# The kv product of a linear attention on 64x32 tiles of TensorE, and a VectorE transpose in place of picking matmuls

## The chip, the cores and the metric

The kernel runs on one core of a Trainium2 chip. The metric is the time of one execution on the device in microseconds, smaller being better. The kernel before took 177.84 us, the median of 3 runs (177.82 to 178.65).

## The reference

Two blocks read the same layer-normalised tokens and are added to the input: a linear attention with a softmax feature map (A) and a small convolutional MLP mixer (B). There are 2048 tokens of 448 numbers, 16 heads of 28, and a hidden width of 1792. All data are bf16.

```python
x  = A_x
xn = layernorm(x)
out = x + A(xn) + B(xn)

# A: per head h of 16, Dh = 28
q, k, v = split(xn @ wqkv)
pq, pk  = q @ w_phi[h], k @ w_phi[h]
phi_q = concat([softmax(pq), softmax(-pq)])     # 56 features
phi_k = concat([softmax(pk), softmax(-pk)])
kv  = phi_k.T @ v                               # 56 x 28 per head, summed over 2048 tokens
z   = phi_k.sum(over tokens)                    # 56 per head
o   = (phi_q @ kv) / (phi_q @ z + 1e-6)
A   = concat_heads(o) @ wo

# B
h  = gelu(layernorm(xn) @ w1)
hs = concat of four channel groups of h, shifted by 1, -1, 2, -2 tokens, @ w2
x1 = xn + hs
B  = x1 + gelu(layernorm(x1) @ w3) @ w4
```

## The kernel before

Tokens lie in 16 tiles of 128. Every operation goes through a recorder: the program calls `R.mm` (TensorE matmul, line 203), `R.act` (ScalarE, line 211), `R.ew` (an elementwise operation on VectorE or GpSimd, line 215) and `R.dma`, in one order written out by hand, and the recorder gives each engine its own instructions in that order and adds a wait where an operand's last writer or reader is another engine. So the hand-written order is the order on each engine; engines run freely against each other between those waits. `solve` (lines 75 to 149) works out the waits; PSUM is tracked by whole banks, of which there are 8, in pairs that `two(b)` reads as one.

Most matmuls contract over 64 rows and come in pairs: one on array rows 0 to 63 (`LO`), one on rows 64 to 127 (`HI`), into two different banks.

The stages, in the order of TensorE's work:

1. Layer norm, transposes of the normalised tokens, v for tiles 0 to 11, the w1 product with gelu, and the folding of `w_phi` into the weights of q and k. This ends with the fold's copies into `wpq`, before 33 us.
2. A loop of eight passes (`ps` 0 to 7, from about 31.4 to 69 us; pass 3 begins at 45.11 us). A pass makes k's features for two token tiles (`k_pair`, banks 2 and 3), q's features for one of 8 blocks (`q_pair`, banks 0 and 1) and one pair of w2 or v tiles (`w2_pair` or `v_pair`, banks 4 and 5). Each of these has a first and a second half on TensorE, called k first, k second and so on below. ScalarE makes the exponentials of k and q (`k_exp`, `q_exp`, two each), VectorE adds the w2 result to the tokens (`w2_out`), sums k's features (`k_norm`: a reduce and a reciprocal) and in some passes makes layer norm statistics (`w2_norm`); GpSimd scales k's features by the reciprocal (the rest of `k_norm`) and applies the second layer norm (`g_apply`).
3. From 68.97 us on, a list that `play` goes through: w3 with gelu for two blocks of 128 hidden columns at a time (`a(p)` its first half, `b(p)` its second), the last w2 tiles, the query products (`N(i)`, with `kvq` as moving operand), w4 and wo, and the stores.

The kv product is what changes. For each token tile, `kv_tile` issues 16 matmuls into banks 6 and 7 (rows `LO` into bank 6, rows `HI` into bank 7). The stationary operand is 128 columns of `phik`, the features of two heads (plus and minus softmax, 32 columns each); the moving operand is the 62 columns of `vaug` that hold the same two heads' v and a column of ones, so half of what comes out pairs a head with its neighbour and is not used. Two token tiles go in each of passes 3 to 7, between k first and w first: that is where 10 of the 16 tiles are. Tiles 10 to 13 come as `K(10, 11, 12, 13)` after `b(1)`, tiles 14 and 15 before `b(3)`. Then `kv_copy` adds the two banks into `kvT`, and `kv_blocks` issues four matmuls with a picking matrix (`pick`, made in `kv_picks` by GpSimd's fill and four VectorE copies) that move the wanted 32-row blocks to the partitions that the query product needs, and four copies (two on VectorE, two on ScalarE) write them to `kvq`.

The first query product, `N(0)`, comes after `a(6)`.

Of the kernel before, what the change touches and what calls it, by code (L numbers as in the profile page):

```python
# [6 lines left out]
ALU = mybir.AluOpType  # L7
AX = mybir.AxisListType
BF16 = mybir.dt.bfloat16
F32 = mybir.dt.float32  # L10
# [7 lines left out]
class Recorder:  # L18
# [56 lines left out]
    def solve(self):  # L75
        pos = {e: 0 for e in self.ENGS}
        known = {e: {} for e in self.ENGS}
        snap = {}
        writers = {}
        readers = {}  # L80
        waits = []
        self.stream = {e: [] for e in self.ENGS}
        ndma = 0
        tiles = {}
        mode = (None, 0)
        for eng, fn, w, r, dma, tile in self.ops:
            me = (eng, pos[eng])
            src = ("D%d" % ndma, 0) if dma else me
            if dma:
                ndma += 1  # L90
            need = {}

            def want(d, raw):
                for f, i in d.items():
                    if f == eng:
                        if eng in ("PE", "SP"):
                            continue
                        if not raw and eng != "POOL":
                            continue
                    if need.get(f, -1) < i:  # L100
                        need[f] = i

            for k in r:
                if k in writers:
                    want(writers[k], True)
                if self.rows[k[0]][1] and k in readers:
                    want({f: i for f, i in readers[k].items() if f != eng}, False)
            for k in w:
                if k in writers:
                    want(writers[k], False)  # L110
                if k in readers:
                    want(readers[k], False)
            if eng == "PE":
                if tile[1] != mode[0]:
                    mode = (tile[1], mode[1] + 1)
                for k in w:
                    for lo, (i, m) in tiles.setdefault(k, {}).items():
                        if lo != tile[0] and m == mode[1]:
                            need["PE"] = max(need.get("PE", -1), i)
                    tiles[k][tile[0]] = (pos["PE"], mode[1])  # L120
            kn = known[eng]
            todo = []
            for f, i in sorted(need.items(), key=lambda t: -t[1]):
                if kn.get(f, -1) >= i:
                    continue
                todo.append((f, i))
                for g, j in snap[(f, i)].items():
                    if kn.get(g, -1) < j:
                        kn[g] = j
                kn[f] = max(kn.get(f, -1), i)  # L130
            todo = [(f, i) for f, i in todo
                    if not any(f2 != f and snap[(f2, i2)].get(f, -1) >= i for f2, i2 in todo)]
            s = dict(kn)
            s[src[0]] = src[1]
            if not dma:
                s[eng] = pos[eng]
            snap[src] = s
            self.stream[eng].append((fn, todo, src, dma))
            waits.extend(todo)
            pos[eng] += 1  # L140
            for k in r:
                readers.setdefault(k, {})[src[0]] = src[1]
            for k in w:
                writers.setdefault(k, {})[src[0]] = src[1]
        self.marked = {}
        for f, i in set(waits):
            self.marked.setdefault(f, []).append(i)
        for f in self.marked:
            self.marked[f] = {i: n + 1 for n, i in enumerate(sorted(self.marked[f]))}
# [74 lines left out]
def bass_parallel_sum__linear_kernel_hedgehog__mixer_s_mlp__prompt_kernel(  # L224
# [13 lines left out]
    with es:  # L238
        R = Recorder(nc, es)
# [9 lines left out]
        def view(h, cols, dt=BF16, at=0):  # L249
            a = h[:, at // 2:at // 2 + cols * DTB[dt] // 2]  # L250
            return a if dt == BF16 else a.bitcast(dt)
# [38 lines left out]
        bd = view(g_r, D)  # L290
        wphi = view(g_r, NC * DH, at=1024).rearrange("p (c f) -> p c f", c=NC)
        kvq = new("kvq", 8 * 64).rearrange("p (b e) -> p b e", b=8)
        kvT = view(w1_r, 512)
        kvf = view(w1_r, 512, F32, at=1024)
        pick = view(w1_r, 2 * 128, at=3072).rearrange("p (s c) -> p s c", s=2)
        ident = new("ident", 128)
        maskb = new("maskb", CR)
        st = new("st", NT * 8, F32).rearrange("p (t c) -> p t c", t=NT)
# [192 lines left out]
        def two(b):  # L491
            return pairs[b // 2].rearrange("p (b e) -> p b e", b=2)
# [3 lines left out]
        def row_pairs(first, second, start=False):  # L496
            for s, (p, q) in enumerate(zip(first, second)):
                for out, lhs, rhs in (p, q):
                    R.mm(out, lhs, rhs, start and s == 0, False)
# [67 lines left out]
            R.ew(dve, "reciprocal", rk, k)  # L567
            R.ew(pool, "tensor_tensor", ph, ph, rk.unsqueeze(2).to_broadcast([128, 4 * H, DH]), op=ALU.mult)

        def kv_tile(i):  # L570
            def side(k, rows):
                return [(banks[6 + k][:, 64 * n:64 * n + HP + DH + 2],
                         phik[rows[0]:rows[1], i, 4 * n:4 * n + 4, :].rearrange("p g e -> p (g e)"),
                         vaug[rows[0]:rows[1], i, 64 * n:64 * n + HP + DH + 2]) for n in range(8)]
            row_pairs(side(0, LO), side(1, HI), i == 0)

        def kv_picks():
            R.ew(pool, "memset", pick[:, :, :], 0.0)
            for q in range(4):
                r = slice(HP * q, HP * q + HP)  # L580
                R.ew(dve, "tensor_copy", pick[r, q % 2, :].rearrange("p (n e) -> p n e", n=4),
                     ident[r, HP * q:HP * q + HP].unsqueeze(1).to_broadcast([HP, 4, HP]))

        def kv_copy():
            n61 = [a.rearrange("p (n e) -> p n e", n=8)[:, :, 0:HP + DH + 2] for a in (banks[6], banks[7], kvf, kvT)]
            R.ew(dve, "tensor_copy", n61[2], n61[0])
            R.ew(dve, "tensor_tensor", n61[3], n61[1], n61[2], op=ALU.add)

        def kv_blocks():
            kt = kvT.rearrange("p (n h e) -> p n h e", n=8, h=2)  # L590
            for s in range(2):
                for k, lo in enumerate((0, 64)):
                    R.mm(banks[6 + k][:, 256 * s:256 * s + 256].rearrange("p (n e) -> p n e", n=8)[:, :, 0:DH + 1],
                         pick[lo:lo + 64, s, :], kt[lo:lo + 64, :, k, 0:DH + 1], s == 0, False)
            for q in range(4):
                r, h, n = slice(HP * q, HP * q + HP), q % 2, 4 * (q // 2)
                src = banks[6 + h][r, :].rearrange("p (s n e) -> p s n e", s=2, n=8)[:, :, n:n + 4, 0:DH + 1]
                dst = kvq[r, :, HP * h:HP * h + DH + 1].rearrange("p (c s) e -> p s c e", s=2)
                if h:
                    R.act(dst, src, ACT.Copy)  # L600
                else:
                    R.ew(dve, "tensor_copy", dst, src)
# [171 lines left out]
                ln_scale(mv2, rs2, i - 2, 4, 4)  # L774

        kv_ones()
        kv_picks()
        side = [("w", 0), ("v", 12), ("w", 2), ("w", 4), ("v", 14), ("w", 6), ("w", 8), ("w", 10)]
        g_at = {2: (0,), 3: (1,), 4: (2, 3), 6: (4,), 7: (5,)}
        for ps in range(8):  # L780
            k, q = k_pair(2 * ps, 1), q_pair(ps // 2, 2 * (ps % 2), 0)
            kind, i = side[ps]
            w = {"w": w2_pair, "v": v_pair}[kind](i, 2)
            k[0]()
            if ps > 2:
                kv_tile(2 * ps - 6)
                kv_tile(2 * ps - 5)
            w[0]()
            k[1]()
            for s in range(2):  # L790
                k_exp(2 * ps, 1, s)
            q[0]()
            w[1]()
            if kind == "w":
                w2_out(i, 2)
            if kind == "v":
                v_out(i, 2, "DVE" if i == 12 else "ACT")
            q[1]()
            for s in range(2):
                q_exp(2 * ps, 0, s)  # L800
            k_norm(2 * ps)
            if kind == "w" and i < 8:
                w2_norm(i)
            for t in g_at.get(ps, ()):
                g_apply(t)
                g_T(t)
# [5 lines left out]
        def a(p):  # L812
            return (w3p[p][0],)

        def b(p):
            return (w3p[p][1],)
# [5 lines left out]
            return (lambda: (num_tile(i), o_T(i)),)  # L822

        def K(*t):
            return (lambda: [kv_tile(i) for i in t],)

        def w2_last(i):
            wl[i][1]()
# [8 lines left out]
        def A(*t):  # L837
# [1 line left out]

        play([  # L840
            A(6, 7), G(6, 7),
            a(0), (wl[12][0],), b(0), a(1), (w2_last, 12), b(1), K(10, 11, 12, 13),
            a(2), (wl[14][0],), b(2), a(3), K(14, 15), b(3), (kv_copy,),
            a(4), (w2_last, 14), b(4), a(5), (kv_blocks,), b(5),
            a(6), N(0), (w2_norm, 8), b(6), a(7), f(1, 0), b(7), N(1), (w2_norm, 10), A(8, 9, 10, 11),
            a(8), f(2, 0), b(8), G(8, 9), a(9), N(2), (w2_norm, 12), b(9),
            a(10), f(3, 0), b(10), f(4, 0), G(10, 11),
# [50 lines left out]
```

## Time and profile before

| | |
|---|---|
| median of 3 runs | 177.84 us |
| span of the profiled execution, first to last instruction | 175.9 us |
| time of that execution beside its span | not recorded by itself; the median lies 1.9 us above the span |
| TensorE (PE) busy | 170.8 us, 97% |
| VectorE (DVE) | 110.0 us, 63% |
| GpSimd (POOL) | 93.7 us, 53% |
| ScalarE (ACT) | 82.5 us, 47% |
| chain of waits that ended last | TensorE 91%, VectorE 6% |
| granted TensorE clock | 0.999 of full speed |

PE is TensorE's matmuls, PEld its weight loads, which run beside them. A matmul's recorded length holds its way through the array: the 62-column matmul is recorded with 188 ns, though the next on the same rows starts after some 28. What a group of matmuls costs is therefore read from the start of the group to the start of the next one, in the timeline. A timeline row gives the start in us, the length in us, the engine, the line, the operation, output and inputs with their shapes, and in brackets how long the engine had stood idle and for whom. In a shape such as `64*128 64x62`, the first part is the rows and columns of the array that are used, the second the moving operand.

### The profile page before, as it was taken

The numbers are of one execution on the slowest core, as the hardware profiler recorded it, in microseconds if no ns is written. First come the engines' busy times: TensorE is split into PE (matmuls) and PEld (weight loads), VectorE is DVE, ScalarE is ACT, GpSimd is POOL, SyncE is SP. The second block draws the span as 40 slices with busy tenths as digits, with TensorE's granted clock in tenths as the row PEclk, the third lists the DMA queues.
The fourth block names the chain that finished last, engine by engine and source line by source line (L and its number), as shares of the span: only waits on it lengthen the run. The fifth ranks groups of instructions, "written<-read, shape, count | busy, mean of one in ns | idle before, by whom it ended". The sixth has DMA issues, their size and how long they took to land.

```text
span 175.9 us, 5042 instructions
## 1 busy us (share of the span) xinstructions
PE 170.8 (97%) x2198; PEld 94.7 (54%) x2198; DVE 110.0 (63%) x252; ACT 82.5 (47%) x92; POOL 93.7 (53%) x130
## 2 busy tenths in 40 slices
PE   7899999998999999999999999999999999999993
PEld 4466557744565555665554554554545545545551
DVE  4799906699899697615776981644427415474621
ACT  2368874997779877926324422223214222224000
POOL 3666670016799999860358489460620723523740
PEclk9999999999999999999999999999999999999999
DMA  5994158990001120121011372134611310311331
GB/s 172 330 240 79 35 97 255 390 345 15 0 4 30 34 60 4 30 55 39 4 34 40 79 74 59 48 82 89 93 30 57 82 34 0 86 30 30 86 100 34
DMA packets 32981, 14.87 MB, mean 85 GB/s; under 512 B 24704, under 2 KB 32448, under 8 KB 32960
## 3 DMA queue, kind: packets, MB, share of 16 engines
q1 hardware_dynamic: 30192, 12.64, 29.6%
q10 hardware_dynamic: 2768, 1.92, 3.4%
q8 instruction: 17, 0.28, 0.7%
q14 instruction: 4, 0.03, 0.1%
HBM read 7.08 MB, written 1.84 MB: 51 GB/s over the span
## 4 chain that ended last, share of the span: by engine, by line
PE 91%; DVE 6%; issue 1%; POOL 0%; ACT 0%; DVEq 0%
PE bank L203 90%; DVE vaug L215 1%; DVE st L215 1%; DVE ksum L215 1%; PE bank L207 1%; DVE xn L215 1%; DVE mv L215 0%; ACT xnT L211 0%; POOL rs L215 0%; DVE rks L215 0%; DVEq L176 0%; DVE gT L215 0%; POOL mv L215 0%
## 5 line engine op out<-in xcount | busy, mean ns | idle before, releaser
L211 ACT ACTIVATE phik<-bank 128x1024 bf16<-128x1024 f32 (+1 forms) x44 | 42.3, 984 | 62.4 <-PE bank L203 62.4
L203 PE MATMUL bank<-gT,w 64*128 64x512 bf16 x392 | 50.1, 377 | 0.0
L215 DVE TENSOR_TENSOR vaug<-bank,vaug 128x464 f32<-128x464 f32 (+3 forms) x65 | 32.6, 512 | 23.0 <-PE bank L203 21.4
L203 PE MATMUL bank<-w,phik 64*128 64x448 bf16 (+1 forms) x420 | 45.0, 349 | 0.0
L215 POOL TENSOR_TENSOR xnT<-vaug 128x196 bf16<-128x196 f32 (+1 forms) x32 | 18.1, 585 | 46.8 <-DVE vaug L215 46.8
L203 PEld LDWEIGHTS bank<-w,phik 64*128 64x128 bf16 (+1 forms) x420 | 21.7, 94 | 21.2 <-issue 0.4
L215 POOL TENSOR_TENSOR phik<-phik,rks 128x1792 bf16<-128x1792 bf16 x8 | 25.7, 3212 | 10.8 <-DVE rks L215 10.8
L203 PEld LDWEIGHTS bank<-gT,w 64*128 64x128 bf16 x392 | 18.6, 94 | 17.0 <-ACT hi L211 0.3
L215 POOL TENSOR_TENSOR vaug<-xn,xtok 128x448 f32<-128x448 bf16 x16 | 16.2, 1031 | 0.2 <-DVE vaug L215 0.2
L215 DVE TENSOR_REDUCE ksum<-phik 128x64 f32<-128x1792 bf16 x8 | 16.0, 2006 | 0.0
L203 PE MATMUL bank<-w,hT 64*128 64x448 bf16 (+1 forms) x128 | 15.0, 349 | 0.5 <-DVE vaug L215 0.5
L215 DVE RECIPROCAL vaug<-bank 128x16 f32<-128x16 f32 x16 | 4.1, 257 | 18.0 <-PE bank L203 18.0
L203 PE MATMUL bank<-xnT,wpq 64*128 64x512 bf16 x112 | 14.9, 376 | 0.0
L203 PE MATMUL bank<-xnT,w 64*112 64x512 bf16 x112 | 14.8, 380 | 0.0
L203 PE MATMUL bank<-wpk,xnT 64*128 64x448 bf16 x112 | 13.4, 349 | 0.0
L203 PE MATMUL bank<-wo,xnT 64*128 64x448 bf16 (+1 forms) x106 | 13.4, 349 | 0.0
L215 DVE TENSOR_TENSOR xn<-bank,xn 128x512 bf16<-128x512 f32 (+1 forms) x16 | 9.2, 616 | 6.3 <-PE bank L203 6.3
L203 PE MATMUL bank<-wv,xnT 64*128 64x448 bf16 x112 | 13.0, 350 | 0.1
L215 POOL TENSOR_TENSOR rs<-mv,mhalf 128x1 f32<-128x1 f32 (+2 forms) x18 | 12.2, 679 | 1.5
L215 POOL TENSOR_SCALAR g_tok<-xn,rs 128x512 bf16<-128x512 bf16 x16 | 12.1, 767 | 0.2
L211 ACT ACTIVATE xnT<-bank 128x512 bf16<-128x512 bf16 x12 | 7.0, 603 | 6.3 <-PE bank L207 6.3
L215 DVE BATCH_NORM_STATS2 st<-xtok 128x6 f32<-128x448 bf16 x16 | 9.8, 615 | 0.0
(62 smaller groups left out, 168.0 us busy)
## 6 DMA issues: line engine op xcount, KB each, us to landing
w<-in_B_w_dram SPq DMA_DIRECT2D x2, 896.0 KB, 7.1
out_dram<-vaug SPq DMA_DIRECT2D x15, 112.0 KB, 1.9
w<-in_B_w_dram SPq DMA_DIRECT2D x1, 1568.0 KB, 12.0
xtok<-in_A_x_dram ACTq DMA_DIRECT2D x2, 448.0 KB, 7.3
xtok<-in_A_x_dram SPq DMA_DIRECT2D x2, 224.0 KB, 5.7
w<-in_B_w_dram ACTq DMA_DIRECT2D x2, 224.0 KB, 5.8
wo<-in_A_wo_dram SPq DMA_DIRECT2D x2, 224.0 KB, 8.4
w<-in_B_w_dram SPq DMA_DIRECT2D x1, 392.0 KB, 3.8
```

The source lines that it names most:

```text
L203: self.op("PE", lambda e: e.matmul(out, lhsT, rhs, start=start, stop=stop, skip_group_check=True), [out], [lhsT, rhs], tile=self._tile(lhsT))
L207: self.op("PE", lambda e: e.transpose(out, in_, ident), [out], [in_, ident], tile=self._tile(in_))
L211: self.op("ACT", lambda e: e.activation(out, in_, func, **kw), [out], [in_] + aps)
L215: self.op(eng, lambda e: getattr(e, name)(out, *args, **kw), [out], aps)
```

## The change

kv is turned round. v of one head (32 columns with the ones) becomes the stationary operand and the features of the head (64 columns, plus and minus) the moving one. The output of a head is then 32 partitions by 64 columns, and the head's place among the four groups of 32 partitions is chosen so that the query product finds it there. A token tile takes 32 matmuls, each on 64 array rows by 32 array columns: eight different such tiles of the array are used in turn (two halves of the rows, four groups of columns). No output is left unused. The 16 token tiles go in two batches: tiles 0 to 11 before `b(0)`, tiles 12 to 15 before `b(3)`; the loop of passes has no kv any more.

The accumulation no longer starts with a flag: VectorE clears banks 6 and 7 before the loop. After the last tile VectorE adds the two banks, transposes the result in blocks of 32x32 (`transpose`, into `kvX`), and four copies, from SBUF now, write `kvq`. The picking matrix and its matmuls are gone. In the recorder, an engine that writes PSUM now also waits for its own earlier reads of that bank; VectorE's clearing is the only instruction that this touches.

```diff
@@ solve
                 if k in readers:
-                    want(readers[k], False)
+                    want(readers[k], self.rows[k[0]][1])
@@ buffers
-        kvT = view(w1_r, 512)
-        kvf = view(w1_r, 512, F32, at=1024)
-        pick = view(w1_r, 2 * 128, at=3072).rearrange("p (s c) -> p s c", s=2)
+        kvT = view(w1_r, 256)
+        kvX = view(w1_r, 256, at=512)
+        kvf = view(w1_r, 256, F32, at=1024)
@@ kv
-        def kv_tile(i):
-            def side(k, rows):
-                return [(banks[6 + k][:, 64 * n:64 * n + HP + DH + 2],
-                         phik[rows[0]:rows[1], i, 4 * n:4 * n + 4, :].rearrange("p g e -> p (g e)"),
-                         vaug[rows[0]:rows[1], i, 64 * n:64 * n + HP + DH + 2]) for n in range(8)]
-            row_pairs(side(0, LO), side(1, HI), i == 0)
-
-        def kv_picks():
-            R.ew(pool, "memset", pick[:, :, :], 0.0)
+        def kv_tiles(tiles):
+            for i in tiles:
+                for s in range(4):
+                    for k, (lo, hi) in enumerate((LO, HI)):
+                        for q in range(4):
+                            h = 8 * (q // 2) + 2 * s + q % 2
+                            R.mm(banks[6 + k][HP * q:HP * q + HP, 64 * s:64 * s + 64],
+                                 vaug[lo:hi, i, HP * h:HP * h + HP],
+                                 phik[lo:hi, i, 2 * h:2 * h + 2, :].rearrange("p g e -> p (g e)"),
+                                 False, False)
+
+        def kv_copy():
+            R.ew(dve, "tensor_copy", kvf, banks[6][:, 0:256])
+            R.ew(dve, "tensor_tensor", kvT, banks[7][:, 0:256], kvf, op=ALU.add)
+            R.ew(dve, "transpose", kvX, kvT)
             for q in range(4):
                 r = slice(HP * q, HP * q + HP)
-                R.ew(dve, "tensor_copy", pick[r, q % 2, :].rearrange("p (n e) -> p n e", n=4),
-                     ident[r, HP * q:HP * q + HP].unsqueeze(1).to_broadcast([HP, 4, HP]))
-
-        def kv_copy():
-            n61 = [a.rearrange("p (n e) -> p n e", n=8)[:, :, 0:HP + DH + 2] for a in (banks[6], banks[7], kvf, kvT)]
-            R.ew(dve, "tensor_copy", n61[2], n61[0])
-            R.ew(dve, "tensor_tensor", n61[3], n61[1], n61[2], op=ALU.add)
-
-        def kv_blocks():
...
-                dst = kvq[r, :, HP * h:HP * h + DH + 1].rearrange("p (c s) e -> p s c e", s=2)
-                if h:
+                dst = kvq[r, :, HP * (q % 2):HP * (q % 2) + DH + 1]
+                src = kvX[r, :].rearrange("p (b e) -> p b e", b=8)[:, :, 0:DH + 1]
+                if q % 2:
                     R.act(dst, src, ACT.Copy)
                 else:
                     R.ew(dve, "tensor_copy", dst, src)
@@ before and in the loop of passes
         kv_ones()
-        kv_picks()
+        R.ew(dve, "memset", two(6)[:, :, 0:256], 0.0)
...
             k[0]()
-            if ps > 2:
-                kv_tile(2 * ps - 6)
-                kv_tile(2 * ps - 5)
             w[0]()
@@ the list that play goes through
-            a(0), (wl[12][0],), b(0), a(1), (w2_last, 12), b(1), K(10, 11, 12, 13),
-            a(2), (wl[14][0],), b(2), a(3), K(14, 15), b(3), (kv_copy,),
-            a(4), (w2_last, 14), b(4), a(5), (kv_blocks,), b(5),
+            a(0), (wl[12][0],), K(*range(12)), b(0), a(1), (w2_last, 12), b(1),
+            a(2), (wl[14][0],), b(2), a(3), K(*range(12, NT)), b(3), (kv_copy,),
+            a(4), (w2_last, 14), b(4), a(5), b(5),
             a(6), N(0), (w2_norm, 8), b(6), a(7), f(1, 0), b(7), N(1), (w2_norm, 10), A(8, 9, 10, 11),
```

More of the change, by code (lines that the diff above doesn't have):

```diff
@@ L589, in kv_blocks @@
-        def kv_blocks():
[L590 to L597, printed above, removed]
-                dst = kvq[r, :, HP * h:HP * h + DH + 1].rearrange("p (c s) e -> p s c e", s=2)
-                if h:
+                dst = kvq[r, :, HP * (q % 2):HP * (q % 2) + DH + 1]
@@ L824, in K @@
         def K(*t):
-            return (lambda: [kv_tile(i) for i in t],)
+            return (lambda: kv_tiles(t),)
         def w2_last(i):
```

## The prediction, before the changed kernel was run

> **What bounds the kernel now.** I read the page first, then the chain of waits, then the groups of instructions by form, then the timeline of the stretch from 43 to 84 us, where all of the change lies. The page and the chain say that TensorE (PE) is the bound, at its full clock:
>
> ```profile
> PE 170.8 (97%) x2198; PEld 94.7 (54%) x2198; DVE 110.0 (63%) x252; ACT 82.5 (47%) x92; POOL 93.7 (53%) x130
> PEclk9999999999999999999999999999999999999999
> ```
>
> ```profile
> 41.51 131.65 PE bank L203 x1716
> ```
>
> From 41.51 us on the chain is PE alone, so a microsecond taken from PE is a microsecond of the kernel, unless PE then stands waiting for an engine that its work had covered. The groups give the forms that the change replaces, and the nearest forms to the new ones (busy us, mean ns of one):
>
> ```profile
> L203 PE MATMUL bank<-vaug,phik 64*128 64x62 bf16 x256 | 4.9, 188 | 0.0
> L203 PEld LDWEIGHTS bank<-vaug,phik 64*128 64x128 bf16 x256 | 4.8, 94 | 1.2
> L203 PEld LDWEIGHTS bank<-xnT,w 64*112 64x112 bf16 x112 | 7.9, 127 | 2.4
> ```
>
> The timeline shows what a kv step costs and who is close behind PE (start, length, engine):
>
> ```profile
> 45.11 0.93 PE L203 MATMUL bank<-wpk,xnT 64*128 64x448 bf16 x8
> 45.87 0.62 PE L203 MATMUL bank<-vaug,phik 64*128 64x62 bf16 x32
> 46.32 0.93 PE L203 MATMUL bank<-w,hT 64*128 64x448 bf16 x8
> ...
> 50.67 0.63 PE L203 MATMUL bank<-vaug,phik 64*128 64x62 bf16 x32
> 51.12 0.93 PE L203 MATMUL bank<-wv,xnT 64*128 64x448 bf16 x8
> ```
>
> ```profile
> 49.69 1.12 DVE L215 TENSOR_TENSOR xn<-bank,xn 128x512 bf16<-128x512 f32 x2
> 50.73 2.01 DVE L215 TENSOR_REDUCE ksum<-phik 128x64 f32<-128x1792 bf16 x1
> ```
>
> ```profile
> 57.08 0.12 PEld L203 LDWEIGHTS bank<-xnT,wpq 64*128 64x128 bf16 x4 [0.28 <-ACT hi L211]
> 57.09 0.39 PE L203 MATMUL bank<-xnT,wpq 64*128 64x512 bf16 x2
> ```
>
> The reader should see three things. 32 kv matmuls (two token tiles) push the next group 0.45 us back, 14.2 ns each, though one is drawn 188 ns long. The wv group at 51.12 starts only 0.31 us after VectorE's add (49.69 to 50.81) has freed its banks; the kv step stood in that gap. And the q group at 57.09 was already held by ScalarE.
>
> The profiled execution is known by its span alone, 175.9 us; the median of the runs is 177.84, so about 1.9 us lie around the span. I work on the span and add the difference to the median. A difference under 0.5% (0.89 us) can hardly be told from none here.
>
> **What PE loses, and what of it is worth something.** Five kv steps of two tiles in the pass loop (passes 3 to 7) are 5 x 0.454 = 2.27 us. K(10 to 13) at 73.50 to 74.41 is 0.91 us, K(14, 15) at 77.54 to 77.99 is 0.45, and the four picking matmuls at 81.77 to 82.03 are 0.25: 3.88 us in all. The last three lie where no PE group waits (each group there starts when the one before has streamed), so their 1.61 us come off in full. The 2.27 us do not, and this is the step I replayed row by row. A pass on PE is k first (0.76), [kv], w or v first (0.76), k second (0.57), q first (0.87), w or v second (0.76, v 0.57), q second (0.64). The w group needs VectorE's add of the pass before, the q group ScalarE's exponentials of the pass before. From the end of a releaser to PE's start I take 0.06 to 0.1 us (57.03 to 57.09; 69.69 to 69.83 is the longest seen).
> - Pass 3: w first can go at 45.93 (the add is 44.67 to 45.83), q first at 47.33 (exponentials end at 47.26) in place of 47.65: 0.32 us gained of 0.45.
> - Pass 4: k first ends at 50.35, but the add at 49.69 does not move, because VectorE comes to it straight from the reduce of 45.74, a reciprocal and the layer norm statistics. The v group goes at 50.91 in place of 51.12: 0.21 gained of 0.91.
> - Pass 5: ScalarE runs k's exponentials, v's copy and q's exponentials in one row from 52.66 to 57.03, and that row starts with k second of pass 4. It moves by 0.21, so q first goes at 56.87: 0.22 gained of 1.36.
> - Pass 6: the add moves from 58.92 to 58.69; w first at 59.95 in place of 60.57 (0.62), q first at 61.34 in place of 61.90 (0.56 of 1.82).
> - Pass 7: VectorE's row from 58.69 (add, reduce, reciprocal, statistics) has no idle time before the add that was at 63.94; it moves by 0.23 and ends at 64.83, w first goes at 64.93 in place of 65.38: 0.45 gained of 2.27.
>
> The gain from all removed work is then 0.45 + 1.61 = 2.06 us, not 3.88: kv was a filler for waits that come back.
>
> **What PE gets.** 512 matmuls of 64 moving columns on tiles of 64 rows by 32 columns, each with its weight load, in batches of 384 and 128. No such tile is in the trace, so I bound it.
> - From below: a round is eight matmuls, four on each half of the rows. If all eight stream together, a round lasts as one pair does now, 28.4 ns for 62 columns, 29.2 for 64. 64 rounds: 1.87 us. The transposes of 64 columns agree: 16 between 18.56 and 18.80 us, 14.6 to 15 ns each.
> - From above: the four column tiles take turns, and every matmul costs the 14.2 ns of today: 7.3 us.
> - Between: the weight loads. 112 columns take 127 ns; 128 columns 94, because (operand field of those instructions) they are read as four runs of 32 where 112 is one run. The 80 steps between are worth 33 ns, 0.41 ns a step, so a load of 32 columns is 13 ns of steps on top of a fixed 81. Four loads now go through the same 64 rows in a round. If their steps can't overlap, a round is 53 ns and the sum 3.4 us. Instructions speak for a middle value as well: the densest stretch of PE shows 128 of them in 0.9 us (73.50), and the first batch alone has 768.
>
> I take 3.4 us: full overlap needs instructions at five times any pace that the trace holds for that long, and no two loads on the same rows are seen closer together than a streamed matmul; against 7.3 us speaks that the two row halves do run at once, and that the loads already run ahead of the matmuls (64 loads from 73.29, their matmuls from 73.50).
>
> [...]
>
> Changing the tile shape: the trace has changes between 64 and 128 rows. From 6.56, eight transposes should stream for 0.12 us, but the next group starts 0.22 us on; the four matmuls of 256 columns after that should take 0.44 and the next group starts after 0.54. That is 0.1 us a change; two batches make four: 0.39 us. A change of columns may cost from nothing to twice that.
>
> **What lies beside.** VectorE's clearing of two PSUM banks takes the place of four copies (0.78 us from 33.40); a fill of 256 elements took 0.27 and one of 768 took 0.70, so 512 lies between, and VectorE waits for PE until 35.38 anyway. GpSimd loses one fill. On VectorE the copy and the add of 496 columns (0.67 each, from 78.20) become 256 columns, with a 32x32 block transpose of 256 columns (bound: 0.1 to 0.7 us by these rows; I take 0.4) and two narrow copies (0.4 each at most), ScalarE two copies of 0.36. That is about 2 us after the last kv matmul; the query needs kvq at 83.55, some 5 us after it, and about 4.4 us of w3 and w2 matmuls cover it. Without that cover it would be up to 1 us. The late batch needs GpSimd's norm of tiles 14 and 15, which ended at 75.50 and can't come much earlier, as GpSimd is full from 48.42; PE comes to it at 77.8 or later, and the first batch needs one that ended at 65.97, against 69.7. So no new wait there. SP's queue and all DMAs are in the same order.
>
> **Sum.** -2.06 + 3.41 + 0.39 = +1.74 us: 179.6 us, a span of 177.6. With the bounds of the new matmuls: +0.2 to +5.6.
>
> **Rivals.**
> - Full overlap. Rounds at 29.2 ns: -2.06 + 1.87 + 0.39 = +0.2, 178.0 us. For it: the two row halves run fully at once today. Against: it needs 768 instructions within 1.4 us.
> - Column tiles in turn, 14.2 ns a matmul: -2.06 + 7.3 + 0.39 = +5.6, 183.5 us. For it: that is the only pace which the trace has held. Against: different array columns, different output partitions.
> - Faster: the loop gives back the whole 2.27 us and rounds stream together: 1.87 + 0.39 - 3.88 = -1.6, 176.2 us. One mechanism, in passes 4 to 7: VectorE's and ScalarE's rows move up with PE. It decides once the loop gains over 1.55 us with full overlap. For it: VectorE still idles for 1.68 us before 58.92 and 0.96 before 68.53. Against: VectorE has no idle time between 44.67 and 57.24, and ScalarE holds pass 5 already.
> - The change doesn't do what it says: all eight tiles in turn, 28.4 ns a matmul, 14.5 us: +12.8, 190.7 us. Against: the row halves run at once today.
>
> **How the numbers follow.** Forecast (new matmuls between 2.6 and 5 us) 0.38, full overlap 0.26, in turn 0.19, faster 0.13, the far end 0.04. The range leaves out the far end and most of the faster case: 177.0 to 183.6 us. Faster by over 0.5% is the faster case, 0.13; within 0.5% is nearly all of full overlap, 0.25; slower is the rest, 0.62.
>
> **What would show it.** In the profile after: the first batch near 69.4 us and how long until the next w3 group (1.4, 2.6 or 5.5 us); its weight loads, about 94 ns each; PE waits for VectorE before the wv group at about 50.9 and for ScalarE at about 56.9; the first w3 group at 68.5. If that group comes at 67.0 or earlier, the replay of the loop is wrong. If the batch of 384 lasts under 1.6 us, the weight loads do overlap, and the forecast is some 1.5 us too high.

## The result, and the profile after

The changed kernel took 188.32 us (median of 4 runs, 187.77 to 189.55) beside 177.94 before: ratio 1.0579, 95% interval 1.0534 to 1.0624. It is 10.4 us slower, where +1.7 was forecast and +5.6 was the far end of the range. The execution whose trace is read here was the longest of the four, 189.55 us, so the account below closes on a somewhat larger change.

The page of the changed kernel: TensorE is still the busiest engine, but at 93% of a span of 187.8 us, and the granted clock has a dip in slices 17 and 18.

```profile
PE 175.3 (93%) x2450; PEld 93.2 (50%) x2450; DVE 109.4 (58%) x250; ACT 82.5 (44%) x92; POOL 93.4 (50%) x129
PEclk9999999999999999759999999999999999999999
```

The timeline of TensorE around the two batches (start, length, form, count, idle time before):

```profile
69.81 0.93 PE L203 MATMUL bank<-w,hT 64*128 64x448 bf16 x8
70.66 1.05 PE L203 MATMUL bank<-phik,vaug 64*32 64x64 bf16 x108
72.01 1.34 PE L203 MATMUL bank<-phik,vaug 64*32 64x64 bf16 x128 [0.30 <-issue]
76.29 1.34 PE L203 MATMUL bank<-phik,vaug 64*32 64x64 bf16 x128 [2.94 <-issue]
80.56 0.35 PE L203 MATMUL bank<-phik,vaug 64*32 64x64 bf16 x20 [2.94 <-issue]
80.84 3.17 PE L203 MATMUL bank<-gT,w 64*128 64x512 bf16 x14
83.81 1.24 PE L203 MATMUL bank<-w,hT 64*128 64x448 bf16 x8
84.88 1.68 PE L203 MATMUL bank<-gT,w 64*128 64x512 bf16 x14
...
88.76 1.22 PE L203 MATMUL bank<-phik,vaug 64*32 64x64 bf16 x128
89.91 1.69 PE L203 MATMUL bank<-gT,w 64*128 64x512 bf16 x14
```

Here is nearly the whole result. The first batch lasts from 70.57 (69.81 and 0.76 of w2) to 80.84: 10.27 us. In it TensorE stands still twice for 2.94 us, and "issue" says that it waits for nothing the profile shows, no other engine and no data. The pieces between the two long stops are 128 matmuls long. 128 matmuls with their 128 weight loads are 256 instructions. Then 14 matmuls of 512 columns take 2.97 us (80.84 to 83.81), which before took 1.51, and 8 of w2 1.07 in place of 0.76: 1.77 us lost to the clock. Four windows show it (after the window and its length: PE busy, PEld, DVE, ACT, POOL, then the granted clock). The clock is at half from 77.61 to 84.44 us, so it fell as the second long stop began; after the first it was still full:

```profile
76.29:77.61 1.32, 1.32 (x128) 1.16 (x128) 0.00 (x0) 0.00 (x0) 1.32 (x2) 1.00 0.10 23
77.61:84.44 6.83, 3.90 (x41) 1.51 (x40) 0.00 (x0) 1.02 (x1) 0.11 (x1) 0.50 0.66 58
80.84:84.88 4.04, 4.04 (x34) 1.52 (x24) 0.00 (x0) 1.02 (x1) 0.00 (x0) 0.55 0.16 37
84.88:95.00 10.12, 10.06 (x212) 4.99 (x210) 4.04 (x9) 5.10 (x7) 0.00 (x0) 1.00 0.01 3
```

The second batch, 256 instructions as well, has no stop: 1.25 us with its tile changes (88.66, where the w3 group before it has streamed, to 89.91).

The same view of the instants in which the batch begins, of the instructions on `phik` alone, shows two paces:

```profile
70.66:70.79 0.13, 0.13 (x32) 0.13 (x33) 0.13 (x1) 0.00 (x0) 0.13 (x1) 1.00 0.00 0
70.88:71.72 0.84, 0.83 (x102) 0.70 (x75) 0.70 (x1) 0.00 (x0) 0.43 (x1) 1.00 0.00 0
```

32 matmuls of 64 columns start in 0.13 us: eight tiles do run together, a round in about 30 ns, where one pair of 62 columns took 28.4. (The count of the second row includes matmuls still running from before.) After these 32, which with their loads are 64 instructions, no matmul starts for 0.10 us (70.79 to 70.89), and from then on the trace's start times are 8.3 ns apart, 67 ns a round; the whole second batch of 128 takes 1.15 us. The fast pace is seen for four rounds at a time only, and with the pause behind them they too come to 56 ns each.

The loop without kv, and VectorE's new work:

```profile
41.99 0.93 PE L203 MATMUL bank<-w,hT 64*128 64x448 bf16 x8 [0.48 <-DVE vaug L215]
51.34 0.93 PE L203 MATMUL bank<-wv,xnT 64*128 64x448 bf16 x8 [0.35 <-DVE xn L215]
57.31 1.04 PE L203 MATMUL bank<-xnT,wpq 64*128 64x512 bf16 x8 [0.30 <-ACT hi L211]
65.34 0.93 PE L203 MATMUL bank<-w,hT 64*128 64x448 bf16 x8 [0.35 <-DVE xn L215]
```

```profile
L215 DVE MEMSET bank<- 128x512 f32 x1 | 0.5, 485 | 0.1
L215 DVE STREAM_TRANSPOSE w<-w 128x256 bf16<-128x256 bf16 x1 | 0.4, 446 | 0.0
```

TensorE waits for VectorE, ScalarE and VectorE again, at the three places where the replay of the passes had put it.

### The profile page after: what moved, and what is told of

Its sections match the earlier page's. It is cut to its first block, busy times and chain, and to the rows that moved or that the text cites. A ratio compares the mean times of both kernels' runs of the same rounds, so it can differ in the third digit from the quotient of the medians.

```text
span 187.8 us, 5543 instructions
## 1 busy us (share of the span) xinstructions
PE 175.3 (93%) x2450; PEld 93.2 (50%) x2450; DVE 109.4 (58%) x250; ACT 82.5 (44%) x92; POOL 93.4 (50%) x129
## 4 chain that ended last, share of the span: by engine, by line
PE 68%; DVE 16%; issue 5%; DMA 4%; ACT 2%; POOL 1%; SPq 1%; ACTq 0%; DVEq 0%
PE bank L203 68%; DVE st L215 5%; DVE xn L215 5%; DVE ksum L215 3%; DMA xtok<-in_A_x_dram 3%; DVE mv L215 2%; DMA xnT<-xn 1%; ACT hi L211 1%; SPq L218 1%; ACT phik L211 1%; POOL rs L215 1%; DVE rks L215 1%; DVE vaug L215 1%; ACTq L221 0%; ACT vaug L211 0%
## 5 line engine op out<-in xcount | busy, mean ns | idle before, releaser
L203 PE MATMUL bank<-gT,w 64*128 64x512 bf16 x392 | 51.3, 386 | 0.1
L203 PEld LDWEIGHTS bank<-gT,w 64*128 64x128 bf16 x392 | 18.1, 95 | 19.2 <-issue 1.4
L203 PE MATMUL bank<-phik,vaug 64*32 64x64 bf16 x512 | 5.3, 198 | 6.2 <-issue 6.2
L203 PEld LDWEIGHTS bank<-w,hT 64*128 64x128 bf16 (+1 forms) x128 | 6.5, 97 | 8.0 <-DVE xn L215 1.8
```

What stands on the lines that cost most here:

```text
L203: self.op("PE", lambda e: e.matmul(out, lhsT, rhs, start=start, stop=stop, skip_group_check=True), [out], [lhsT, rhs], tile=self._tile(lhsT))
```

## The experiments

To compare traces whose start differs by some tenths of a us, I count from the w2 group that waits for VectorE's v copy (41.51 before, 41.99 after, the same event in all) to the first w3 group, and to the first query matmul. Before, these are 27.46 and 42.04 us; in the changed kernel 26.96 and 53.46. From the first query matmul to the end all traces agree within 0.03 us (92.34 to 92.37). So all of the change, +11.42 us in this execution, lies between the two marks (the marks themselves come 0.48 us later than before).

**Theory of instruction supply:** TensorE gets its instructions in pages of 256, as many as lie between its stops at 72.01, 76.29 and 80.56, and the next page comes while TensorE is on the one before it; where it is through before the next one is there, it stands still. **Rival, tile shape:** the 32-column tiles, or their weight loads, stop the array. The profiles count the packets on the instruction queue, before and in the changed kernel (packets, MB, share of time):

```profile
q8 instruction: 17, 0.28, 0.7%
q8 instruction: 19, 0.31, 0.7%
```

That is 16 KB each, so 64 bytes an instruction if a packet is a page of 256. The counts fit TensorE: its matmuls and loads are 4396 before, 4900 in the changed kernel and 3876 in the kernel without kv of experiment 4, and 256 goes into these 17.2, 19.1 and 15.1 times; that last kernel has 15 packets. In the changed kernel's trace the packets begin at 69.69, 73.46, 78.28 and 81.79 us, where before they began some 7 to 12 us apart. The first three end at 70.61, 74.84 and 79.24 us, and TensorE goes on at 72.01, 76.29 and 80.56: 1.3 to 1.45 us after each. In the other kernels with stops this is 1.2 to 1.4 us. That a page comes one ahead is seen at the first of these: TensorE passes matmul 728, 128 before the first stop, at 68.51 us; the packet begins 1.2 us later, and TensorE works on without it until behind matmul 856. The other three begin 1.2 to 2.0 us after TensorE has gone on with a new page (72.01, 76.29, 80.56). In the kernel before there are 17 packets and 17 such counts (88, 216 and so on to 2136), and from 40 us on each packet begins within 22 matmuls of one.

**1. The same matmuls, spread over the old places.**

```diff
@@ changed kernel, loop of passes
             k[0]()
+            if ps > 2:
+                kv_tiles((2 * ps - 6, 2 * ps - 5))
             w[0]()
@@ list
-            a(0), (wl[12][0],), K(*range(12)), b(0), a(1), (w2_last, 12), b(1),
-            a(2), (wl[14][0],), b(2), a(3), K(*range(12, NT)), b(3), (kv_copy,),
+            a(0), (wl[12][0],), b(0), a(1), (w2_last, 12), b(1), K(10, 11, 12, 13),
+            a(2), (wl[14][0],), b(2), a(3), K(14, 15), b(3), (kv_copy,),
```

> The changed kernel with its 64x32 matmuls put back where kv stood before: two token tiles in each of passes 3 to 7, then tiles 10 to 13, then 14 and 15. Theory of instruction supply (TensorE gets its instructions in pages of 256, one page ahead, and a page takes some 4.3 us to follow the last, as between 72.01, 76.29 and 80.56 us): no step asks for more than a page, so the stalls of 2.9 us are gone and the time is 178.5 to 180 us. What is left over the kernel before is the pace: 64 matmuls take about 0.5 us and two tile changes 0.2, against 0.45. Rival, the tile shape (something in the 32-column tiles or their weight loads stops the array every 128 matmuls): the stalls stay in number, 186 us or more.

Measured 179.81 us, ratio 1.0092 (1.0063 to 1.0121). All 512 matmuls on 32-column tiles are there, no stop is, and the clock stays at full. The rival as stated, a stop every 128 matmuls, has fallen. A step of two tiles:

```profile
66.21 0.68 PE L203 MATMUL bank<-phik,vaug 64*32 64x64 bf16 x64
66.83 0.93 PE L203 MATMUL bank<-w,hT 64*128 64x448 bf16 x8
```

From the end of k first (65.36 + 0.76) to 66.83 it takes 0.71 us, where the 64x128 form took 0.45. Five times 0.26 are the 1.3 us by which the loop is longer (28.78 for 27.46). So even without a stop the new form is the dearer one.

**2. The old matmuls in the new batches.**

```diff
@@ kernel before, loop of passes
-            if ps > 2:
-                kv_tile(2 * ps - 6)
-                kv_tile(2 * ps - 5)
@@ list: K(*range(12)) before b(0), K(*range(12, NT)) before b(3), as in the changed kernel
```

> The kernel before with its own 64x128 kv matmuls, put into the two batches of the changed kernel (tiles 0 to 11 before b(0), 12 to 15 before b(3)). The loop then gains only about 0.5 us and the batches cost 3.6 where 1.4 stood, so +1.8 us without any stall: 179.7 us. Instruction supply: the first batch is 384 instructions in 2.7 us, more than a page, so one stall of 0.5 to 2.5 us comes on top: 180.2 to 182.3 us, with TensorE idle inside the batch. Tile shape: no stall, 179.7 us.

Measured 179.55 us, ratio 1.0073 (1.0049 to 1.0097).

```profile
70.06 2.89 PE L203 MATMUL bank<-vaug,phik 64*128 64x62 bf16 x192
72.78 1.68 PE L203 MATMUL bank<-gT,w 64*128 64x512 bf16 x14
```

192 matmuls in 2.72 us, 14.2 ns each, with no stop. Here my expectation from instruction supply was wrong in its detail: 384 instructions are more than a page, but when the batch began some 216 were left of the page in use (that is where the changed kernel stopped first, after 108 matmuls), and at 14.2 ns a matmul these last 1.5 us, about until the next page was there. So this run does not tell the two theories apart. By this account how far a burst gets depends on where in a page it begins: the changed kernel's first batch had 108 matmuls left and stopped behind them for 0.30 us, the second had 50 left and crossed over at 89.13 us without a stop. The loop's account is exact: the first w3 group comes at 26.96 us, and to the first query it is 43.79, +1.75, which is -0.50 for the loop, -1.36 for the late steps and +3.62 for the batches.

**3. The old tile shape with the new number of instructions.** The decisive one.

```diff
@@ experiment 2, kv_tile
-                return [(banks[6 + k][:, 64 * n:64 * n + HP + DH + 2],
+                return [(banks[6 + k][:, 64 * n + 31 * c:64 * n + 31 * c + 31],
...
-                         vaug[rows[0]:rows[1], i, 64 * n:64 * n + HP + DH + 2]) for n in range(8)]
+                         vaug[rows[0]:rows[1], i, 64 * n + 31 * c:64 * n + 31 * c + 31]) for n in range(8) for c in range(2)]
```

> As the run with 64x128 kv in two batches, but each kv matmul is cut into two of 31 moving columns, so that it has as many TensorE instructions as the changed kernel (768 and 256) and no 32-column tile. Instruction supply: stalls of about 2.9 us each as in the changed kernel and a slow clock after them, 186 to 190 us. Tile shape: no stall; 512 matmuls at 8 to 14 ns are 4.3 to 7.3 us in place of 3.6, so 180.4 to 183.4 us.

Measured 188.39 us, ratio 1.0572 (1.0515 to 1.0629): the changed kernel's time, without one 32-column tile.

```profile
70.67 3.18 PE L203 MATMUL bank<-vaug,phik 64*128 64x31 bf16 x236
75.51 1.89 PE L203 MATMUL bank<-vaug,phik 64*128 64x31 bf16 x128 [1.66 <-issue]
79.23 0.45 PE L203 MATMUL bank<-vaug,phik 64*128 64x31 bf16 x20 [1.84 <-issue]
79.53 3.04 PE L203 MATMUL bank<-gT,w 64*128 64x512 bf16 x14
```

The two long stops come after the same matmul numbers as in the changed kernel: 236 is 108 + 128, then 128, then 20 are left. They are shorter, since the matmuls of a page take longer, but the period is about the same: 75.51 to 79.23 is 3.7 us (4.27 in the changed kernel). The packets on the instruction queue begin at 69.15, 72.88, 76.63 and 80.40: 3.75 us apart. So a page in some 3.75 to 4.3 us is what TensorE was given in these two kernels, 15 to 17 ns an instruction, 29 to 33 ns for a matmul with its load. The slow clock comes here too, from 75.50 to 82.32 us, after the first of the two stops.

**4. No kv matmuls at all** (`for s in range(0)` in `kv_tiles`).

> The changed kernel with all kv matmuls left out, so that kv is zero; all else is as in it. It measures what taking kv out of the loop is worth. By the replay of the passes the removed work gives 0.5 us in the loop and 1.6 us after it: 175.8 us. If the loop gave back all that is taken out: 3.9 us, 174.0 us.

Measured 176.66 us, ratio 0.9907 (0.9871 to 0.9943). The loop gives back 0.50 us (26.96 for 27.46) of the 2.27 taken out; the replay said 0.45. From the first w3 group to the first query it gives back only 1.13, not 1.61. Where the rest went is seen in experiment 1 as well:

```profile
82.35 3.42 PE L203 MATMUL bank<-gT,w 64*128 64x512 bf16 x28
...
84.09 1.19 PEld L203 LDWEIGHTS bank<-gT,w 64*128 64x128 bf16 x14 [0.55 <-PE bank L203]
...
85.61 0.39 PE L203 MATMUL bank<-kvq,eq_lo 64*128 64x62 bf16 x16
```

28 matmuls take 3.26 us where 28 at 0.1075 are 3.01. `b(5)` now follows `a(5)` directly; its two row halves write each other's banks, and the recorder makes it wait until `a(5)` is through the array: about 0.22 us, which the picking matmuls had covered. In experiment 4 `a(3)` and `b(3)` lie together too: twice 0.22 are the 0.44 of the missing 0.48.

**5 and 6. A shorter first batch**, with the other tiles two by two in the last passes (`if ps > 5`, `K(*range(4, 12))`; then `if ps > 3`, `K(*range(8, 12))`).

> The changed kernel with tiles 0 to 3 moved back into passes 6 and 7, two in each, so that the first batch has 8 tiles, 512 instructions. Instruction supply: the batch is one page shorter, so one of the two stalls of 2.9 us goes, and with it the 1.1 us of that page's matmuls; 0.7 us for each step in a pass come back, in part into waits. 183 to 185.5 us, and less if the clock no longer drops. A cost for each batch, whatever its length (a change of the tile mode gone wrong), would leave 188 us.

> As the run with 8 tiles in the first batch, but tiles 0 to 7 go into passes 4 to 7 and the batch has 4 tiles, 256 instructions. Instruction supply: no stall of 2.9 us is left and the clock stays up, 179.5 to 180.8 us. A cost for each batch: 188 us.

Measured 186.35 us, ratio 1.0431 (1.0357 to 1.0504), and 180.58, ratio 1.0128 (1.0095 to 1.0160).

```profile
71.90 2.41 PE L203 MATMUL bank<-phik,vaug 64*32 64x64 bf16 x236
76.64 0.35 PE L203 MATMUL bank<-phik,vaug 64*32 64x64 bf16 x20 [2.34 <-issue]
```

With 8 tiles one stop is left, after number 236 again; with 4 none over 0.3 us. That is the step by pages. The first of the two missed its range by 0.85 us, because the clock cost more, not less: 28 w3 and 8 w2 matmuls after the stop took 6.58 us (76.92 to 83.50) where before they took 3.78. The half clock lasted as long as in the changed kernel (75.78 to 82.60 us, 6.8 us), but TensorE worked through 6.0 us of it, where the changed kernel stood still in much of it and worked 3.9.

**7. The same 1024 instructions in the same stretch, in four pieces** (4 tiles each before `b(0)`, `b(1)`, `b(2)` and `b(3)`).

> The changed kernel with the first batch cut into three of 4 tiles (before b(0), before b(1), before b(2)), each followed by 14 to 16 long matmuls, the last batch as it was. All 1024 kv instructions still come between 70 and 83 us. Instruction supply: four batches of 1.15 us and eight tile changes are about +2.9 us over the kernel before, 180.9 us, and the long matmuls give the next page time, so that stalls are short: 180.9 to 183 us. A cost of 2.9 us for every 128 matmuls on 32-column tiles would leave 188 us or more.

Measured 183.88 us, ratio 1.0313 (1.0278 to 1.0349), above the range. The second, third and fourth piece:

```profile
74.54 0.87 PE L203 MATMUL bank<-phik,vaug 64*32 64x64 bf16 x86
75.85 0.50 PE L203 MATMUL bank<-phik,vaug 64*32 64x64 bf16 x42 [0.45 <-issue]
...
78.66 0.68 PE L203 MATMUL bank<-phik,vaug 64*32 64x64 bf16 x64
79.58 0.68 PE L203 MATMUL bank<-phik,vaug 64*32 64x64 bf16 x64 [0.24 <-issue]
...
81.81 0.57 PE L203 MATMUL bank<-phik,vaug 64*32 64x64 bf16 x50
83.31 0.80 PE L203 MATMUL bank<-phik,vaug 64*32 64x64 bf16 x78 [0.93 <-issue]
```

The stops are 0.45, 0.24 and 0.93 us, and the clock stays up, but the four pieces take 7.05 us in all, not 5.0. The long matmuls in between hid a good part of the supply (1.62 us of stops where the changed kernel had 6.18), not all: the stretch still asks for 1140 instructions in some 13 us, one in 11.4 ns, where a page was given at 15 to 17 ns an instruction.

This trace holds the plainest sign of the pages. Between two pieces lie 14 w3 and 8 w2 matmuls, between the last two 14 w3. From the first stop to the second TensorE starts 42 + 14 + 8 + 64 = 128 matmuls, from the second to the third 64 + 14 + 50 = 128, with their loads 256 instructions each time, whatever their form; and the stops come 3.73 us apart. Counted from the program's first matmul, all nine stops of over 0.2 us in the kv batches, in four kernels, stand behind matmul 856 (changed kernel), 984 (changed kernel, split kernel, this one), 1112 (all four) or 1240 (this one).

No version here that computes kv beats the kernel before, and the accounts point to none: kv in the loop costs 0.5 us net for 2.27 us of work, and the new form is dearer step by step.

## Why the prediction was wrong, step by step

**Right.** The loop: 0.45 us predicted, 0.50 measured in the changed kernel, in experiment 4 and in all others without kv in the loop; its waits came at the places named, counted from the same event within 0.1 us. The faster rival, that the loop gives back everything, is refuted by the same number. The sign of the result: the terms named in the sum carry it without the stops and the clock (about +2.9 us, worked out below). The cover of VectorE's tail: clearing took 0.49 us, the transpose 0.45 (0.4 taken), and the first query matmul waited for none of it.

**Wrong, the term of the new matmuls.** This is the step that failed. It stood as 3.41 us with 0.39 for tile changes, out of a choice between three prices, and all three looked at the array; what it costs to supply TensorE with instructions stood at nothing. Measured, against the forecast of +1.74:
- For four rounds the array shows the lowest of the three prices: about 30 ns a round where the rival of full overlap had 29.2. In these rounds the weight loads, on which I placed the forecast, do not queue on their row half: 33 of them lie in the 0.13 us of the 32 matmuls, each recorded with 89 ns on average, where my estimate had 94.
- Beyond the first 32 matmuls it is 8.3 ns for a matmul and its load, 67 ns a round where the forecast had 53. As the same form ran faster just before, I take this pace to be set in front of the array; no run shows that by itself. Both batches with their changes come to 5.34 us without the stops (10.27 - 6.18 + 1.25) in place of 3.80: +1.54. Some 0.55 us of this belong to the three stops, since the last matmul before each is counted with its whole recorded length of 0.2 us; the two batches without stops would then take 4.8 us, and the whole sum would be +2.9.
- The stops: 0.30 + 2.94 + 2.94 = 6.18 us. They were in no case of the prediction. I had written that 128 instructions in 0.9 us were the densest stretch of the trace and that the batch had 768, and took it as an argument for a middle value; a resource that the trace has never been seen to deliver should have been a rival with its own price. What the trace of before did hold were the packets on the instruction queue, one for about 256 instructions.
- The clock: 1.77 us, also in no case.
- The picking matmuls: counted as 0.25 in full, worth 0.03, because they covered TensorE's wait for itself: +0.22.

1.74 + 1.54 + 6.18 + 1.77 + 0.22 - 0.05 (loop) = 11.40; the traces differ by 11.42.

**What the runs show of the supply.** They show the blocks: stops at the same counts in four kernels, multiples of 256 instructions apart. And they show that TensorE stood still for the next one, for up to 2.94 us, where it issued an instruction in 4.2 ns.

**Open.** That the slow clock is a consequence of the stops is argued, not shown by itself: it came in the three kernels with stops of 1.66 us or more and in none with stops of 0.93 us or less, but no run kept the stops and took the clock drop away. How long a stop it takes is open too: in the changed kernel the clock was still full after the first stop of 2.94 us, in the split kernel it fell as one of 1.66 ended. And what sets the pace of 8.3 ns is inferred, as said above.

## What to carry to other kernels

Count instructions, not only array time: where a change cuts work into more and shorter TensorE instructions, compare instructions per microsecond with the densest stretch the trace has sustained over a whole page of 256, and give the shortfall a price of its own. Before crediting removed work in full, look for what waits behind it within its own length, on other engines and on the same engine's own results: here 2.27 us in the loop were worth 0.50, and 0.25 us of picking were worth 0.03. The form that was as fast as hoped in the array for four rounds (30 ns each) was slower in a stream (0.71 us a step for 0.45), so try a new form first where the old one stands, and move it afterwards.

## What the runs showed of the hardware that was not expected

- TensorE's supply of instructions: a page of 256 in 3.7 to 4.3 us when it is asked for without pause, after 472 instructions (236 matmuls and their loads) with no stop over 0.30 us. The changed kernel, the split kernel and the one with 8 tiles stop after exactly the same 236 matmuls, and in the interleaved one the stops are 128 matmuls of mixed forms apart.
- Between the stops, 4.2 ns an instruction on the 32-column tiles; in the first 64 of a batch, and again behind the stops that end at 72.01 and 76.29, faster still (32 matmuls and their loads in 0.13 us), with a pause of 0.10 us behind them.
- Halving the moving columns from 62 to 31 on 64x128 tiles hardly made a matmul cheaper: 128 of them took 1.64 us (86.94 to 88.58 in experiment 3), 12.8 ns each, where 62 columns took 14.2.
- In the three kernels with stops of 1.7 to 2.9 us the granted clock went to half for 6.8 us, each time once (14 matmuls of 512 columns in 2.97 us in place of 1.51). This cost 1.4 to 2.8 us, about as much as a stop.
